# A first layer's weights narrowed by two VectorE instructions with ScalarE's sign, their range check moved into the second layer

## The chip, the core and the metric

One core of a Trainium2 chip runs the whole program. The engines are TensorE (PE; its weight loads, which overlap with the matmuls, are listed as PEld), VectorE (DVE), ScalarE (ACT), GpSimd (POOL) and SyncE (SP), which here only issues DMAs. A q behind an engine's name is its instruction queue. The metric is the time of one execution in microseconds (us).

## What is computed

Complex decaying linear attention over 4 batches, 8 heads, 768 steps and a head size of 48, and then two gated feed-forward layers over the 3072 resulting rows of 384, each with 1536 hidden units; the second normalises its input first.

```
a_re_n, a_im_n = a_re * scale, a_im * scale      # |a| held to 0.999
S_t = a_t * S_(t-1) + k_t v_t^T ;  y_t = q_t . Re(S_t)
x1 = (silu(x @ w_gate) * (x @ w_val)) @ w_out
xn = x1 / sqrt(mean(x1^2) + 1e-6) * rms_g
out = (silu(xn @ w2_gate) * (xn @ w2_val)) @ w2_out
```

The weights come as float64. The kernel takes each as two 32-bit words, makes the float32 number of them ("narrowing"), and splits that into two halves for TensorE, so that a product of two numbers takes three matmuls.

## The kernel before

The sequence is cut into six blocks of 128 steps (512 rows with the four batches). For a block, `e1` and `scan` make the running products of the decays for four heads (a pair of groups), `back`, `e2a` and `e2b` apply them to q and k, and `pe_att` lets TensorE do the transposes (`tp`), scores (`sp`), outputs (`yp`) and the state's update (`zp`) of a group of two heads. When a block's four groups are done, `split_x` splits its rows into `xh` and `xl`, and `layer1` runs the first gated layer on it.

A gated layer goes over 12 blocks of 128 hidden units (`ffn_items`): 9 matmuls into a `gv` buffer for the gate, silu on ScalarE into `h` (line 369), 9 matmuls for the value, the product on VectorE (378), its high half `hh` on ScalarE (379), the low half `hl` on VectorE (387), and then the output's matmuls (`acc` in layer 1, line 792; `o` in layer 2, line 912), one hidden block behind. The `gv` buffers are three.

A hidden block has three weight tiles of 128x384 (gate, value, out), and `load_w` (line 319) prepares each: SP loads the words into `wraw` (two buffers, line 327), `narrow` makes `wy` with three VectorE instructions (lines 59 to 61), ScalarE copies the high half (330) and does the range check, a Square and a Relu that each add up what they find into `wstat` (331, 332). The low half comes from TensorE in layer 1 (`wl`, lines 335 and 336, then a copy, 337) and from VectorE in layer 2 (339). Layer 1's 36 tiles are prepared while the attention of the first blocks runs; layer 2's during the last block of layer 1 and the first of layer 2, since most wait for the space of layer 1's.

The order of the work in the first part is set by due times: each task (`e` for the decays of a pair, `b` for the work on q and k of a group, `t` for its TensorE part, `x` and `f` for split and layer 1 of a block, `w` for a weight tile) has a start and a length in the tables at the top, and `in_order` sorts all items by them. A scheduler then places each engine's instructions, with a priority for the silu, product and halves (`HP`). At the end, `wstat` and other statistics decide whether the plain recurrence has to be run instead (it isn't).

## Time and profile before

| what | value |
|---|---|
| three timed runs, median (range) | 1218.65 us (1217.30 to 1219.31) |
| the profiled execution, span from its first to its last instruction | 1218.1 us |
| TensorE busy | 1136.6 us (93%) |
| its weight loads busy | 945.7 us (78%) |
| VectorE busy | 772.5 us (63%) |
| ScalarE busy | 668.2 us (55%) |
| mean granted TensorE clock | 0.979 of full |

The profiled execution's time outside the span is not listed. A share of busy time is a mean over stages that differ; a line such as "PE wl L335 <- DVE wy L61" says that TensorE's `wl` matmul of line 335 waited for the VectorE instruction of line 61 that writes `wy`.

### The profile page before, as it was taken

The numbers are of one execution on the slowest core, as the hardware profiler recorded it, in microseconds if no ns is written. First come the engines' busy times: TensorE is split into PE (matmuls) and PEld (weight loads), VectorE is DVE, ScalarE is ACT, GpSimd is POOL, SyncE is SP. The second block draws the span as 40 slices with busy tenths as digits, with TensorE's granted clock in tenths as the row PEclk, the third lists the DMA queues.
The fourth block names the chain that finished last, engine by engine and source line by source line (L and its number), as shares of the span: only waits on it lengthen the run. The fifth ranks groups of instructions, "written<-read, shape, count | busy, mean of one in ns | idle before, by whom it ended". The sixth has DMA issues, their size and how long they took to land.

```text
span 1218.1 us, 16677 instructions
## 1 busy us (share of the span) xinstructions
PE 1136.6 (93%) x6098; PEld 945.7 (78%) x6098; DVE 772.5 (63%) x1703; ACT 668.2 (55%) x1159; POOL 1.5 (0%) x12
## 2 busy tenths in 40 slices
PE   2368979999999999999999999999999999999997
PEld 1256767788888888888878887888888888888886
DVE  5997989989898696888754488742422424224222
ACT  5666979877677656675464688742421424214211
POOL 0000000000000000000000000000000000000000
PEclk9877989999999999999999999999999999999999
DMA  6355454432423224232313244400010000000000
GB/s 166 87 138 145 120 151 124 141 110 74 107 77 101 72 63 119 57 85 67 98 59 97 79 130 145 128 26 27 1 52 1 26 26 1 26 1 1 27 1 29
DMA packets 105514, 90.84 MB, mean 75 GB/s; under 512 B 34000, under 2 KB 92368, under 8 KB 105424
## 3 DMA queue, kind: packets, MB, share of 16 engines
q1 hardware_dynamic: 102832, 84.97, 24.8%
q10 hardware_dynamic: 2592, 4.72, 1.0%
q8 instruction: 50, 0.82, 0.3%
q14 instruction: 40, 0.33, 0.1%
HBM read 66.06 MB, written 18.87 MB: 70 GB/s over the span
## 4 chain that ended last, share of the span: by engine, by line
PE 72%; ACT 11%; DVE 8%; DMA 5%; issue 1%; SPq 1%; ACTq 0%; DVEq 0%
PE gv L360 39%; PE o L912 12%; PE acc L792 8%; PE sp L699 4%; PE tp L684 3%; DMA wraw<-in_moe_w_gate_dram 2%; ACT T L690 2%; PE zp L740 2%; PE yp L716 2%; DMA wraw<-in_moe_w_val_dram 2%; PE yp L721 1%; ACT w L331 1%; ACT L420 1%; ACT T L687 1%; ACT w L332 1%
## 5 line engine op out<-in xcount | busy, mean ns | idle before, releaser
L360 PE MATMUL gv<-xh,w 128*128 128x512 f32 x1728 | 571.4, 396 | 0.3 <-ACT h L369 0.3
L360 PEld LDWEIGHTS gv<-xh,w 128*128 128x128 f32 x1728 | 324.6, 188 | 68.7 <-issue 2.1
L360 PE MATMUL gv<-xl,w 128*128 128x512 f32 x864 | 339.5, 393 | 0.0
L378 DVE TENSOR_TENSOR gv<-h,gv 128x512 f32<-128x512 f32 x144 | 99.8, 693 | 225.5 <-PE gv L360 219.5
L369 ACT ACTIVATE h<-gv 128x512 f32<-128x512 f32 x144 | 85.7, 595 | 187.3 <-PE gv L360 186.8
L360 PEld LDWEIGHTS gv<-xl,w 128*128 128x128 f32 x864 | 162.6, 188 | 32.4 <-issue 1.7
L379 ACT ACTIVATE hh<-gv 128x512 fp32r<-128x512 f32 x144 | 85.5, 594 | 166.4 <-DVE gv L378 166.2
L387 DVE TENSOR_TENSOR hl<-gv,hh 128x512 fp32r<-128x512 f32 x144 | 99.1, 688 | 102.3 <-PE o L912 72.5
L792 PE MATMUL acc<-hh,w 128*128 128x512 f32 x432 | 149.0, 399 | 2.4 <-ACT hh L379 2.4
L912 PE MATMUL o<-w,hh 128*128 128x384 f32 x576 | 146.4, 336 | 0.2 <-ACT x1s L798 0.2
L912 PEld LDWEIGHTS o<-w,hh 128*128 128x128 f32 x576 | 105.6, 188 | 5.7 <-ACT x1s L798 0.5
L912 PE MATMUL o<-w,hl 128*128 128x384 f32 x288 | 96.9, 340 | 0.5 <-DVE hl L387 0.5
L792 PEld LDWEIGHTS acc<-hh,w 128*128 128x128 f32 x432 | 80.3, 188 | 21.3 <-ACT hh L379 4.3
L792 PE MATMUL acc<-hl,w 128*128 128x512 f32 x216 | 86.3, 399 | 0.7 <-DVE hl L387 0.7
L335 PE MATMUL wl<-wy,ident 128*128 128x384 f32 x72 | 39.1, 632 | 43.7 <-DVE wy L61 31.5
L690 ACT ACTIVATE T<-tp 96x512 f32<-96x512 f32 x48 | 52.6, 1097 | 43.0 <-PE tp L684 42.6
L699 PEld LDWEIGHTS sp<-T,T 96*128 96x128 f32 x384 | 51.0, 202 | 24.1 <-ACT T L687 22.6
L699 PE MATMUL sp<-T,T 96*128 96x128 f32 x384 | 56.9, 294 | 11.0 <-ACT T L687 10.7
L912 PEld LDWEIGHTS o<-w,hl 128*128 128x128 f32 x288 | 53.6, 188 | 2.6 <-DVE hl L387 2.6
L335 PEld LDWEIGHTS wl<-wy,ident 128*128 128x128 f32 x72 | 14.2, 228 | 51.8 <-DVE wy L61 36.4
L369 ACT ACT_TABLE_LOAD x38 | 48.8, 1283 | 3.4 <-PE gv L360 2.7
L792 PEld LDWEIGHTS acc<-hl,w 128*128 128x128 f32 x216 | 40.6, 188 | 11.1 <-DVE hl L387 2.8
(131 smaller groups left out, 1496.4 us busy)
## 6 DMA issues: line engine op xcount, KB each, us to landing
wraw<-in_moe_w_gate_dram SPq DMA_DIRECT2D x24, 384.0 KB, 3.5
wraw<-in_moe_w_val_dram SPq DMA_DIRECT2D x24, 384.0 KB, 3.5
wraw<-in_moe_w_out_dram SPq DMA_DIRECT2D x24, 384.0 KB, 3.1
kd<-kt SPq DMA_DIRECT2D x24, 384.0 KB, 2.6
ktok<-kd SPq DMA_DIRECT2D x24, 384.0 KB, 3.5
aar<-in_a_re_dram SPq DMA_DIRECT2D x48, 96.0 KB, 2.3
aar<-in_a_im_dram SPq DMA_DIRECT2D x48, 96.0 KB, 2.6
qk<-in_q_dram SPq DMA_DIRECT2D x96, 48.0 KB, 2.4
```

Source lines behind the costliest of these rows:

```text
L335: T.matmul(ps[:, :384], ident, y, start=True, stop=False)
L360: T.matmul(ps[:, :N], w[:, a, i + c, :], x()[b][:, c, :N], start=(n == 0), stop=(n == 8))
L369: A.activation(h[:, :N], st[f, 0][:, :N], AF.Silu)
L378: V.tensor_tensor(t[:, :N], st[f, "h"][:, :N], st[f, 3][:, :N], op=ALU.mult)
L379: A.activation(hh[:, :N], t[:, :N], AF.Copy)
L387: V.tensor_tensor(hl[:, :N], st[f, "t"][:, :N], st[f, "hh"][:, :N].bitcast(F32), op=ALU.subtract)
L684: T.transpose(ps[0:96, u * 128:u * 128 + 128], s[:, u, h].rearrange("p c d -> p (c d)"), ident)
L690: A.activation(t[:, :N].rearrange("p (b r u) -> p u b r", u=U, b=B), ps[0:96, :N].rearrange("p (u b r) -> p u b r", u=U, b=B), AF.Copy)
L699: T.matmul(ps[:C, bb * C:bb * C + C], o[h, 1][:, bb], o[h, 0][:, :, bb, :], start=True, stop=True)
L716: T.matmul(dst, vt[i][:C, col:col + 64], o[h, "p"][:C, bb * C:bb * C + C].rearrange("p (u r) -> p u r", u=U), start=True, stop=not inter)
L792: T.matmul(acc[e][:, :N], w[:, a, 6 + e, :], hs_[c][:, :N], start=(f == 0 and n == 0), stop=(f == NF - 1 and n == 2))
L912: T.matmul(acc[m][:, :DM], hs_[c][:, m * 128:m * 128 + 128], w[:, a, 6:9, :].rearrange("p c e -> p (c e)"), start=(f == 0 and x == 0), sto ...
```

## The change

For layer 1's weights `narrow2` takes the place of `narrow`. ScalarE takes the Sign of the upper word, read as a float, and scales it by -2.0; VectorE then shifts the lower word in with an exclusive or, and the upper word likewise, in two instructions (lines 69 and 70) where there were three. This holds for weights in a known range, which the check has to ascertain.

Layer 1's range check leaves `load_w`. In layer 2, from its second block on, each silu is followed by one check (`check_w`: Square, Relu and a second Relu, each with an accumulated sum), until all 36 tiles are through; for it each tile is loaded a second time (`check_load`), into the `wraw` buffers that are then free. One added VectorE instruction joins the second sum to the first. Layer 2's weights keep `narrow` and their check, which now stands ahead of the high half's copy.

The tables of due times, two lengths, the two priorities (`HP`, `HP_AT`), the place of a late item (`ZAT`), the moment of the first normalisation (`XAT`), that of layer 2's weights (`LAG`), and one table-load setting (`LOGS2`) have new values. Comments are gone.

```
-T_E1 = [-0.615, 0.377, 2.51, 3.055, 4.01, 5, 6.095, 7.158, 8, 9, 10, 10.197]
+T_E1 = [-0.615, 0.377, 2.51, 3.055, 3.906, 5, 6.095, 7.158, 8, 8.14, 10, 10.197]
...
-D_E1 = 1.023
-D_E2 = 1
+D_E1 = 0.801
+D_E2 = 1.049
...
-ZAT = 6
-HP = 140
-HP_AT = 0
+ZAT = 3
+HP = 166
+HP_AT = 33
...
+def narrow2(A, V, raw, y, sg):
+    lo, hi, yu = raw[:, :, 0], raw[:, :, 1], y.bitcast(U32)
+    A.activation(sg, hi.bitcast(F32), AF.Sign)
+    A.activation(sg, sg, AF.Copy, scale=-2.0)
+    V.scalar_tensor_tensor(yu, lo, 29, sg.bitcast(U32), op0=ALU.logical_shift_right, op1=ALU.bitwise_xor)
+    V.scalar_tensor_tensor(yu, hi, 3, yu, op0=ALU.logical_shift_left, op1=ALU.bitwise_xor)
...
+        def range_of(up, lo, dst, n):
+            A.activation(dst, up, AF.Square, accum_out=wstat[:, 0, n:n + 1])
+            A.activation(dst, lo, AF.Relu, scale=-1.0 / LOW ** 2, bias=one, accum_out=wstat[:, 1, n:n + 1])
...
+        def check_w(raw, n):
+            a, t = raw[:, :, 0].bitcast(F32), raw[:, :, 1].bitcast(F32)
+            A.activation(a, t, AF.Square, accum_out=wstat[:, 0, n:n + 1])
+            A.activation(t, a, AF.Relu, scale=-1.0 / LOW ** 2, bias=one, accum_out=wstat[:, 1, n:n + 1])
+            A.activation(t, a, AF.Relu, bias=high, accum_out=wbig[:, n:n + 1])
...
-                    narrow(V, raw, y)
+                    if layer == 0:
+                        narrow2(A, V, raw, y, y)
+                    else:
+                        narrow(V, raw, y)
+                        range_of(raw[:, :, 1].bitcast(F32), lo.bitcast(F32), lo, n)
                     A.activation(hi, y, AF.Copy)
-                    A.activation(lo, raw[:, :, 1].bitcast(F32), AF.Square, accum_out=wstat[:, 0, n:n + 1])
-                    A.activation(lo, lo.bitcast(F32), AF.Relu, scale=-1.0 / LOW ** 2, bias=one, accum_out=wstat[:, 1, n:n + 1])
...
-                fn()
+                r = fn()
+                if n and r is not None:
+                    if ready:
+                        with tc.issue_after(r.ins):
+                            check_w(*ready.pop(0))
...
+                    if todo:
+                        m = todo.pop(0)
+                        ready.append((check_load(m), m))
```

Lines of the changed kernel lie about 32 further down: 486 to 489 are the running products' instructions (454 to 457 before), 363 and 368 the copies of the high half and of `wl` (330 and 337), 400 the silu, 411 the copy to `hh`, 719 and 722 the copies of `tp` (687 and 690), 735 the masked scores `pt` (703).

On VectorE, around the 13th and the 14th narrowed tile, shortly before layer 1's first matmul. Before:

```order
L494 SCALAR_TENSOR_TENSOR e1w_848<-an_847,e1w_848 128x768
L60 SCALAR_TENSOR_TENSOR wy_899<-wraw_900,wy_899 128x384
L59 TENSOR_SCALAR wy_924<-wraw_925 128x384
L61 SCALAR_TENSOR_TENSOR wy_899<-wraw_900,wy_899 128x384
L60 SCALAR_TENSOR_TENSOR wy_924<-wraw_925,wy_924 128x384
L703 TENSOR_TENSOR pt_838<-sp_833,mask4_99 128x512
L499 SCALAR_TENSOR_TENSOR e1w_848<-e1w_848,an_847 128x768
L778 TENSOR_TENSOR xl_917<-xf_506,xh_916 128x512
L502 TENSOR_TENSOR an_847<-aar_714,e1w_848 128x768 x2
L703 TENSOR_TENSOR pt_863<-sp_858,mask4_99 128x512
L747 TENSOR_SCALAR state_108<-zp_867 96x384
L61 SCALAR_TENSOR_TENSOR wy_924<-wraw_925,wy_924 128x384
```

Now:

```order
L486 TENSOR_TENSOR sc1_904<-an_804 128x384
L70 SCALAR_TENSOR_TENSOR wy_892<-wraw_893,wy_892 128x384
L735 TENSOR_TENSOR pt_831<-sp_826,mask4_99 128x512
L779 TENSOR_SCALAR state_108<-zp_833 96x384
L487 TENSOR_TENSOR sc2_905<-an_804 128x384
L782 TENSOR_TENSOR state_108<-state_108,zp_833 96x384
L488 TENSOR_TENSOR an_804<-sc1_904,sc2_905 128x192
L489 TENSOR_TENSOR an_804<-sc1_904,sc2_905 128x192
L810 TENSOR_TENSOR xl_911<-xf_499,xh_910 128x512 x2
L69 SCALAR_TENSOR_TENSOR wy_918<-wraw_919,wy_918 128x384
L735 TENSOR_TENSOR pt_870<-sp_865,mask4_99 128x512
L70 SCALAR_TENSOR_TENSOR wy_918<-wraw_919,wy_918 128x384
```

Each tile has two instructions (69 and 70) in place of three; the split of the block's rows (778, now 810) and the state's update (750, now 782) stand ahead of the 14th tile now, and so does the first part of a running product (486 to 489).

On ScalarE at the same place, around the preparation of the 14th tile. Before:

```order
L330 ACTIVATE w_898<-wy_899 128x384
L690 ACTIVATE T1_845<-tp_840 96x4x128
L687 ACTIVATE T0_855<-tp_850 96x512
L337 ACTIVATE w_898<-wl_908 128x384
L331 ACTIVATE w_898,wstat_63<-wraw_954 128x384
L332 ACTIVATE w_898,wstat_63<-w_898,small_92 128x384
L330 ACTIVATE w_898<-wy_924 128x384
L723 ACTIVATE yt_894<-yp_885 128x512
```

Now:

```order
L67 ACTIVATE wy_918<-wraw_919 128x384
L363 ACTIVATE w_891<-wy_892 128x384
L68 ACTIVATE wy_918<-wy_918 128x384
L722 ACTIVATE T1_853<-tp_848 96x4x128
L368 ACTIVATE w_891<-wl_900 128x384
L719 ACTIVATE T0_860<-tp_855 96x512
L67 ACTIVATE wy_946<-wraw_947 128x384
L68 ACTIVATE wy_946<-wy_946 128x384
L363 ACTIVATE w_891<-wy_918 128x384
```

The check (331, 332) is gone; a Sign (67) and a scaled copy (68) stand ahead of the tile's high half, with copies for the attention and for earlier tiles between them.

On ScalarE in layer 2, at the beginning of its second block. Before:

```order
L369 ACTIVATE h_8065<-gv_8055 128x512
L379 ACTIVATE hh_8077<-gv_8067 128x512
L369 ACTIVATE h_8092<-gv_8082 128x512
L379 ACTIVATE hh_8104<-gv_8094 128x512
L369 ACTIVATE h_8135<-gv_8125 128x512
L379 ACTIVATE hh_8147<-gv_8137 128x512
```

Now:

```order
L400 ACTIVATE h_8062<-gv_8052 128x512
L342 ACTIVATE craw_8035,wstat_63<-craw_8035 128x384
L343 ACTIVATE craw_8035,wstat_63<-craw_8035,small_92 128x384
L344 ACTIVATE craw_8035,wbig_6675<-craw_8035,high_6673 128x384
L411 ACTIVATE hh_8079<-gv_8069 128x512
L400 ACTIVATE h_8110<-gv_8100 128x512
L342 ACTIVATE craw_8067,wstat_63<-craw_8067 128x384
L343 ACTIVATE craw_8067,wstat_63<-craw_8067,small_92 128x384
L344 ACTIVATE craw_8067,wbig_6675<-craw_8067,high_6673 128x384
L411 ACTIVATE hh_8127<-gv_8117 128x512
L400 ACTIVATE h_8154<-gv_8144 128x512
```

Between a silu (400) and the copy to `hh` (411) stand the three instructions of a check on a tile loaded again (`craw`). On SP the first two of these loads stand ahead of the load of the next block's rows, the third behind the four stores of the first block's output, and the others one by one between the later loads and stores.

## Rows read from the trace of the kernel before

**Rows 1.** The page, busy us, share of the span and instructions of each engine.

```profile
PE 1136.6 (93%) x6098; PEld 945.7 (78%) x6098; DVE 772.5 (63%) x1703; ACT 668.2 (55%) x1159; POOL 1.5 (0%) x12
```

**Rows 2.** Busy time by stage (A to E in order): stretch, length, engines, clock, DMA, GB/s.

```profile
0.00:115.40 115.40, 60.18 (x295) 41.94 (x296) 91.92 (x231) 72.23 (x152) 1.32 (x11) 0.82 0.47 129
115.40:245.00 129.60, 118.00 (x652) 91.88 (x652) 120.65 (x315) 107.86 (x225) 0.00 (x0) 0.97 0.49 137
245.00:683.50 438.50, 434.44 (x2685) 360.08 (x2685) 339.01 (x789) 276.77 (x390) 0.20 (x1) 1.00 0.30 84
683.50:790.00 106.50, 103.41 (x459) 84.96 (x459) 85.64 (x173) 85.96 (x210) 0.00 (x0) 1.00 0.44 130
790.00:1218.10 428.10, 420.55 (x2013) 366.86 (x2012) 135.26 (x199) 125.36 (x184) 0.00 (x0) 1.00 0.05 17
```

**Rows 3.** Waits of TensorE in A: total us, times, longest.

```profile
PE wl L335 <- DVE wy L61: 28.8, 7, 13.9
```

**Rows 4.** Waits of TensorE in B.

```profile
PE tp L684 <- DVE X L457: 5.9, 1, 5.9
...
PE wl L335 <- DVE wy L61: 2.7, 2, 1.6
...
PE sp L699 <- ACT T L687: 0.9, 3, 0.3
```

**Rows 5.** Groups by line: shapes, count, busy us, mean ns, idle us before and releaser.

```profile
L387 DVE TENSOR_TENSOR hl<-gv,hh 128x512 fp32r<-128x512 f32 x144 | 99.1, 688 | 102.3 <-PE o L912 72.5 <-ACT hh L379 15.2 <-PE acc L792 14.0
...
L332 ACT ACTIVATE w<-w,small 128x384 fp32r<-128x384 f32 x72 | 44.0, 611 | 0.9
...
L60 DVE SCALAR_TENSOR_TENSOR wy<-wraw,wy 128x384 uint32<-128x384 uint32 x72 | 39.6, 552 | 0.8
...
L331 ACT ACTIVATE w<-wraw 128x384 fp32r<-128x384 f32 x72 | 39.5, 549 | 12.9 <-DMA wraw<-in_moe_w_gate_dram 6.4 <-DMA wraw<-in_moe_w_val_dram 5.2 <-DMA wraw<-in_moe_w_out_dram 1.0
...
L59 DVE TENSOR_SCALAR wy<-wraw 128x384 uint32<-128x384 uint32 x72 | 25.4, 355 | 18.6 <-DMA wraw<-in_moe_w_gate_dram 12.6 <-DMA wraw<-in_moe_w_val_dram 3.5 <-DMA wraw<-in_moe_w_out_dram 2.2
...
L454 DVE TENSOR_TENSOR sc<-X 128x180 f32<-128x180 f32 (+5 forms) x84 | 25.2, 300 | 1.1
...
L454 DVE TENSOR_TENSOR sc<-an 128x384 f32<-128x384 f32 x36 | 19.8, 551 | 0.3
...
L331 ACT ACTIVATION_READ_ACCUMULATOR w<-wraw 128x1 f32 x72 | 13.9, 193 | 0.0
...
L456 DVE TENSOR_TENSOR an<-sc,sc 128x192 f32<-128x192 f32 x24 | 8.4, 350 | 0.1
```

**Rows 6.** VectorE at the second and third narrowing: start us, us, instruction.

```profile
18.29 0.35 DVE L59 TENSOR_SCALAR wy<-wraw 128x384 uint32<-128x384 uint32 x1
18.56 0.55 DVE L61 SCALAR_TENSOR_TENSOR wy<-wraw,wy 128x384 uint32<-128x384 uint32 x1
```

**Rows 7.** ScalarE around a table load.

```profile
703.62 0.51 ACT L330 ACTIVATE w<-wy 128x384 fp32r<-128x384 f32 x1
704.14 1.28 ACT L369 ACT_TABLE_LOAD   x1
705.44 0.60 ACT L369 ACTIVATE h<-gv 128x512 f32<-128x512 f32 x1
```

**Rows 8.** ScalarE in layer 2, a silu and the copy behind it.

```profile
850.90 0.60 ACT L369 ACTIVATE h<-gv 128x512 f32<-128x512 f32 x1 [2.85 <-PE gv L360]
853.68 0.60 ACT L379 ACTIVATE hh<-gv 128x512 fp32r<-128x512 f32 x1 [2.18 <-DVE gv L378]
```

**Rows 9.** The chain that ended last, in layer 2: start us, us, what.

```profile
832.19 8.20 PE gv L360 x36
...
903.56 4.46 PE o L912 x24
...
1205.96 4.48 PE o L912 x24
```

**Rows 10.** DMA issues: count, KB each, median us to landing.

```profile
wraw<-in_moe_w_gate_dram SPq DMA_DIRECT2D x24, 384.0 KB, 3.5
```

More of the change, by code (lines that the diff above doesn't have):

```diff
@@ L24 @@
 UNITS = [4, 4, 4, 4, 4, 4]
-T_E1 = [-0.615, 0.377, 2.51, 3.055, 4.01, 5, 6.095, 7.158, 8, 9, 10, 10.197]
+T_E1 = [-0.615, 0.377, 2.51, 3.055, 3.906, 5, 6.095, 7.158, 8, 8.14, 10, 10.197]
 T_A = [-0.251, 0.965, 2.01, 2.555, 3.95, 4.95, 5.95, 6.95, 7.95, 8.084, 9.939, 10.147]
-T_E2 = [0.533, 1.547, 2.901, 3.934, 4.547, 5.547, 6.547, 6.742, 7.742, 8.742, 9.742, 9.939]
-T_AT = [1.042, 1.872, 3.207, 4.24, 5.042, 5.317, 6.918, 8.042, 9.236, 10.042, 10.704, 10.987]
+T_E2 = [0.533, 1.547, 2.901, 3.934, 4.547, 5.458, 6.547, 6.742, 7.742, 8.742, 9.742, 9.939]
+T_AT = [1.06, 1.877, 3.225, 4.258, 5.06, 5.335, 6.936, 8.06, 9.254, 10.06, 10.722, 11.005]
 T_F = [2.9, 5.616, 7.11, 9.343, 11.118]
-T_X = [2.85, 4.956, 6.956, 8.956, 10.956]
-D_E1 = 1.023
-D_E2 = 1
+T_X = [2.85, 4.956, 6.956, 11.192, 13.192]
+D_E1 = 0.801
+D_E2 = 1.049
 D_AT = 1
 D_F = [2.386, 3.063, 1.974, 1.954, 2.623]
-ZAT = 6
-HP = 140
-HP_AT = 0
+ZAT = 3
+HP = 166
+HP_AT = 33
 BUFS = dict(kt=2, e2t=1, ktok=1, T1=1, T0=2, qt=1, X=1, Xt=2, Ttok=1, qk=2, vt=2, pt=2, md=1, h=1, hh=2, hl=1, yt=2, wy=2, wraw=2)
 EARLY = 1
-LAG = 0.51
-XAT = 3.312
+LAG = 0.5
+XAT = 3.731
 LOGS1 = 2
-LOGS2 = 3
+LOGS2 = 2
 PROD = 1
@@ L314, in decay_attention_two_ffn, with check_load @@
             masks[u] = m
+        def range_of(up, lo, dst, n):
+            A.activation(dst, up, AF.Square, accum_out=wstat[:, 0, n:n + 1])
+            A.activation(dst, lo, AF.Relu, scale=-1.0 / LOW ** 2, bias=one, accum_out=wstat[:, 1, n:n + 1])
+        def check_load(n):
+            raw = wst.tile([128, 384, 2], U32, tag="wraw", name="craw", bufs=BUFS["wraw"])
+            dst = raw.rearrange("p n t -> p (n t)")
+            f, i = divmod(n, 3)
+            SY.dma_start(out=dst if i == 2 else dst.rearrange("p (c f) -> p c f", c=NC),
+                         in_=words((wg, wv, wo)[i], f, i == 2))
+            return raw
+        def check_w(raw, n):
[3 more added lines that the diff above has]
+            A.activation(t, a, AF.Relu, bias=high, accum_out=wbig[:, n:n + 1])
         def load_w(w, srcs, f, layer, which=(0, 1, 2)):
@@ L368, in go @@
                     with tc.high_priority(HP):
-                        A.activation(h[:, :N], st[f, 0][:, :N], AF.Silu)
+                        r = A.activation(h[:, :N], st[f, 0][:, :N], AF.Silu)
                     st[f, "h"] = h
+                    return r
                 return go
@@ L931, in decay_attention_two_ffn @@
         G.memset(ones, 1.0)
+        high = ff2.tile([128, 1], F32, name="high", bufs=1)
+        G.memset(high, -3.9999997)
+        wbig = ff2.tile([128, 3 * NF], F32, name="wbig", bufs=1)
         wx = fast.enter_context(tc.tile_pool(name="wx", bufs=EARLY))
@@ L957, in decay_attention_two_ffn @@
             nf_ += 1
+        todo, ready = list(range(3 * NF)) if wg.dtype == U32 else [], []
         for n in range(nb_):
@@ L963, in decay_attention_two_ffn @@
                     x2[n + 1] = norm(512 * (n + 1))
-                fn()
+                r = fn()
[3 more added lines that the diff above has]
+                            check_w(*ready.pop(0))
+                        if not ready and not todo:
+                            V.tensor_tensor(wstat[:, 1, :3 * NF], wstat[:, 1, :3 * NF], wbig, op=ALU.add)
+                    if todo:
+                        m = todo.pop(0)
+                        ready.append((check_load(m), m))
     with tc.tile_pool(name="fl", bufs=1) as fl_, tc.tile_pool(name="fps", bufs=1, space=PSUM) as fps:
```

## The prediction

> **What bounds the kernel now.** Over the whole span TensorE is busy 93% and VectorE 63% [rows 1]. That average hides stages, so I read the busy time by stage next [rows 2]. Stage A (0 to 115.4 us) ends with the first matmul of layer 1, B (to 245 us) covers the rest of the first block of layer 1 and the last of its weights, C (to 683.5) the other blocks, D (to 790) the loading of layer 2's weights, E the rest. TensorE's idle time is the stage less its busy time: A 115.4 - 60.2 = 55.2 us, B 129.6 - 118.0 = 11.6, C 438.5 - 434.4 = 4.1, D 106.5 - 103.4 = 3.1, E 7.6, all of it behind the last matmul, since the chain of waits runs through layer 2 on TensorE alone and its last matmul ends at 1205.96 + 4.48 = 1210.4 [rows 9]. So from 245 us on the kernel is TensorE's, and time can be won nearly only in A and B, 66.8 us of idle time.
>
> Who keeps TensorE waiting there? In A its waits for a narrowed weight (`wy`, line 61) are the largest item, 28.8 us in 7 waits [rows 3]; VectorE is busy 91.9 of 115.4 us [rows 2]. In B VectorE is busy 120.7 of 129.6 us, TensorE 118.0 and ScalarE 107.9 [rows 2]: VectorE is the densest, TensorE close behind. TensorE's listed waits in B end with VectorE for the most part: 5.9 (line 457), 2.7 (the narrowing), against 0.9 for ScalarE's copies [rows 4].
>
> **What the change moves, and its price.** *VectorE.* Each of layer 1's 36 weights loses the 0.355 us instruction of line 59; the two that remain have the form of line 60, 0.552 us [rows 5]. That is 36 x 0.355 = 12.8 us. The true gain of one lies between 0.27 (the distance from its start to the next start when it runs back to back, 18.29 to 18.56 [rows 6]) and 0.355: 9.7 to 12.8 us for all. I take the upper end, because line 60 needs its result and often stands next to it.
>
> The due times are new, so I compare VectorE's order up to the same two instructions. Up to the 14th narrowing (both orders put 14 weights ahead of layer 1's first matmul): 14 x 0.355 = 5.0 us less, but one more step of running products (lines 454 to 457, 2 x 0.55 + 2 x 0.35 = 1.8 us [rows 5]) and two small ones (lines 750 and 546, at most 1.1, I take 0.7) more: **-2.5 us**. Up to the 36th: 12.8 less, ten of the running products' instructions more (at most 0.30 each, 3.0) and one 0.69 us subtraction (line 387) less [rows 5]: -12.8 + 3.0 - 0.7 = **-10.5 us**, so -8.0 of it in B. The matmuls ahead of these points are the same but for about one attention step.
>
> A then starts layer 1 earlier by 2.5 us (between 0, if another chain than VectorE's ends last, and 5.0). In B VectorE's 120.7 us fall to 112.7, below TensorE's 118.0. The two change places, so not all 8.0 can be kept: VectorE will wait more for TensorE. The floor is 118.0 plus the waits that ScalarE causes (0.9 and some tenths), about 119.5, so at most 129.6 - 119.5 = 10 us could go; I take three quarters of 8.0, **-6.0** (ends 0 and -10).
>
> *ScalarE.* A weight's range check (lines 331 and 332 with two reads of the accumulator, 0.549 + 0.611 + 2 x 0.193 = 1.55 us) goes, Sign and a scaled Copy come. No row shows Sign on this form; the nearest are Copy on 128x384 (0.51 [rows 7]) and Square (0.549 [rows 5]); I take 0.52 for each, as both are near the Copy: 1.04 us, so 36 x 0.5 = 18 us less (17 to 19 by the two ends). The new order has 6 more table loads (90 for 84), 5 of them ahead of the 12th silu. A load takes 1.28 us and the next instruction starts 1.30 us after it, while the one ahead ended as it began (703.62 + 0.51, then 704.14 [rows 7]): 6 x 1.3 = 7.8 us. ScalarE is left with about 10 us less in A and B, so I cost this at nothing. The Trainium skill says it otherwise ("ScalarE: Activation LUTs", section What ACT_TABLE_LOAD costs): a switch is the load and a drain of about 1.38 us, 2.66 in all. By that, six would cost 16 us and ScalarE would be left with some 2 us less; the sum would stay, with no cushion. The rows here show no drain, and I go by them. The Sign, however, stands ahead of VectorE's first narrowing instruction, a new wait (a rival below).
>
> *Layer 2's weights (D).* The range check moves ahead of the high half's copy, and can run while VectorE narrows. The work is the same; at stake are the 3.1 us of idle time. I take 0 (ends -3 and +2).
>
> *The check in layer 2 (E).* It adds 36 loads of 384 KB on SP (3.5 us to landing [rows 10]) and 108 instructions behind 36 silus of the layer's second to fifth block, about 0.549 + 2 x 0.611 + 3 x 0.193 = 2.35 us each time. Queued behind them on ScalarE is the copy to `hh`. Now it starts 853.68 - 850.90 = 2.78 us after the silu starts, 2.18 us after it ends, because VectorE's product comes first [rows 8]. So `hh` is late by at most 0.2 us, and its matmuls come only after the next 18 `gv` matmuls, 4.1 us (half of the 8.20 for 36 [rows 9]). At a block's end there is no such cover (24 `o` matmuls in a row [rows 9]), but 12 of the 24 still come first, half of 4.46 us. Each load is issued about two silus ahead, 12 us, except behind the output's stores at a block's end. Cost: 0. If that cover failed, the three block ends that have checks on both sides would lose up to a landing each, 3 x 3.5 = 10.5 us.
>
> **Sum.** -2.5 - 6.0 = -8.5 us. The profiled execution's span is 1218.1 us; the median of the runs shown is 1218.65, 0.6 more, with what lies around the span. The sum is set against the latter: 1218.65 - 8.5 = **1210.2 us**. I call no change what is within 0.2% (2.4 us).
>
> **Rivals.** *1. TensorE is the bound already, and nothing is gained.* TensorE's 118.0 us in B are 91% of the stage, and its longest wait there, 5.9 us, is one stall in the attention chain [rows 4], which shorter narrowing need not shorten. Then only the 2.7 us of B's waits for narrowed weights shrink, by a quarter (0.355 of 1.46): 1218.0 us. The Trainium skill argues this way ("Perfetto Trace Analysis", section Identifying the Most-Contended Engine): work first on the engine with the highest occupancy, judging TensorE by its weight loads; over the span these are busy 78%, VectorE 63%. The same page allows for regimes in which the engine changes. Against the rival stand the narrowing's 28.8 us in A [rows 3] and VectorE's 93% of B [rows 2]. Chance 0.17.
>
> *2. Sign holds up VectorE, and it gets slower.* ScalarE runs in order, with 107.9 of B's 129.6 us busy, and a Sign that stands behind a late copy or a late load makes VectorE, the densest engine, wait. The gain is gone when a weight's narrowing waits 0.355 us longer on average. With half of Sign and Copy exposed (0.52) it is 36 x (0.52 - 0.355) = +5.9 us: 1224.6 us; all exposed, +24.7. For it: both are new links in the chain from load to narrowed weight, 1.04 us against the 0.355 saved. Against it: in the new order VectorE has other work between most of them, and Sign needs only the load, as the Square of line 331 did, and a free `wy` buffer, as line 59 did. Chance 0.09.
>
> *3. The check's loads come late in layer 2* and give the gain back, up to 10.5 us as above: 1210.2 + 10.5 = 1220.7 us. Chance 0.04.
>
> **How the numbers follow.** The forecast, VectorE's relief shows in A and B, has 0.70. Its ends are -5.0 - 10 = -15 (1203.7 us) and a loss of most of it (about 1215). The range goes from there up to 1217.5, past the forecast's end into the first rival; what is left out is the rest of the three rivals and the tail below, some 2 in 10. Faster: the forecast and 0.06 of rival 1 (with part of B's gain) and 0.02 of rival 3, 0.78. Same: 0.10 of rival 1 and 0.01 each of 2 and 3, 0.12. Slower: 0.08 of rival 2, 0.01 each of 1 and 3, 0.10.
>
> **What would show it.** Right: the first `gv` matmul of layer 1 starts at about 113 us, the last narrowing ends some 8.5 us earlier than now, VectorE's share of B falls below TensorE's, and from there to the end every stage keeps its length. The instructions that take the place of lines 60 and 61 show about 0.55 us, Sign and Copy about 0.52, and no table load stands in front of a Sign. Layer 2's blocks still take 75.8 us each (from 832.19 to 903.56 + 4.46 [rows 9]), with no hole on TensorE. Wrong: VectorE's narrowing waits for ScalarE by more than 0.355 us a weight; the first matmul comes no earlier; holes in front of `o` matmuls at the block ends; or TensorE's idle time of B reappears in C, in front of the attention's matmuls.

## The result, and the profile after

| | before | after |
|---|---|---|
| timed runs, median (range), us | 1218.49 (1217.30 to 1219.31), 4 runs | 1236.52 (1234.94 to 1237.57), 4 runs |
| ratio after to before, 95% interval | | 1.0142 [1.0122, 1.0163] |

The change makes the kernel 18.0 us slower, where 8.5 us less were forecast; the range ended at 1217.5. The page after, busy time by engine:

```profile
PE 1150.9 (93%) x6098; PEld 950.7 (77%) x6098; DVE 766.2 (62%) x1668; ACT 739.5 (60%) x1309; POOL 1.6 (0%) x13
```

VectorE does less work (772.5 to 766.2 us, with 36 instructions fewer and one more, beside [rows 1]). TensorE has the same 6098 matmuls and is busy 14.3 us longer. To see where, here is the busy time by stage after, cut at the matmuls of [rows 2] (B's end within 0.7 us, D's within 1.4) (stretch, length, TensorE, weight loads, VectorE, ScalarE, GpSimd, clock, DMA share, GB/s):

```profile
0.00:121.85 121.85, 65.12 (x294) 45.28 (x295) 91.90 (x224) 70.79 (x123) 1.32 (x11) 0.96 0.45 125
121.85:250.60 128.75, 116.68 (x649) 91.11 (x649) 115.34 (x292) 106.44 (x181) 0.00 (x0) 0.97 0.48 136
250.60:697.00 446.40, 441.39 (x2689) 362.53 (x2688) 337.09 (x783) 280.11 (x397) 0.24 (x2) 1.00 0.29 82
697.00:805.30 108.30, 105.22 (x468) 86.41 (x467) 85.67 (x170) 86.24 (x211) 0.00 (x0) 1.00 0.44 135
805.30:1235.40 430.10, 422.50 (x2005) 365.42 (x2003) 136.22 (x202) 195.96 (x399) 0.00 (x0) 0.99 0.15 48
```

A is 6.5 us longer, though VectorE is no busier in it; B only 0.9 us shorter (1.6 by the same matmul), though VectorE has 5.3 us less; C 7.9 us longer (8.6 by the same matmul) with hardly more idle time, 5.0 us for 4.1; D and E together 3.8 us longer.

*A.* TensorE's idle time there is 56.7 us after and 55.2 before, 1.5 more; its busy time is 4.9 us more. The waits in A, of TensorE before (beside [rows 3]), then of TensorE and VectorE after (engine, line, what was waited for, total us, times, longest):

```profile
PE wl L335 <- DVE vt L449: 12.1, 1, 12.1
...
PE tp L684 <- DVE kt L659: 3.9, 3, 3.1
PE tp L684 <- ACT T L690: 1.2, 1, 1.2
```

```profile
PE wl L366 <- DVE wy L70: 37.6, 7, 16.4
PE tp L716 <- DVE kt L691: 7.5, 3, 3.9
...
PE tp L716 <- ACT T L722: 4.9, 4, 1.5
...
DVE wy L69 <- ACT wy L68: 4.0, 3, 2.6
```

By these names TensorE's wait for narrowed weights rose from 28.8 us [rows 3] to 37.6. But TensorE's very first wait, for the first weight, is listed before under `vt` (12.1 us) and after under `wy` (13.4 us). Counted alike, the wait is 40.9 us before and 37.6 after: it became 3.3 us shorter, as it was to. What rose is the wait of the attention's transposes, for `kt` and for ScalarE's copies `T`, from 5.1 to 12.4 us. TensorE in the middle of A, before and then after (start us, us, instruction, idle time before it):

```profile
60.83 1.97 PE L716 MATMUL yp<-pt,vt 128*64 128x128 f32 x14 [1.18 <-DVE pt L703]
...
70.82 1.06 PE L684 MATMUL tp<-ident,kt 128*96 128x128 f32 x4
...
74.47 1.16 PE L699 MATMUL sp<-T,T 96*128 96x128 f32 x8 [1.13 <-ACT T L687]
75.47 0.80 PE L740 MATMUL zp<-vt,ktok 128*96 128x48 f32 x8
```

```profile
58.15 1.97 PE L748 MATMUL yp<-pt,vt 128*64 128x128 f32 x14 [0.17 <-DVE pt L735]
...
72.31 1.41 PE L772 MATMUL zp<-vt,ktok 128*96 128x48 f32 x8
...
77.17 1.06 PE L716 MATMUL tp<-ident,kt 128*96 128x128 f32 x4
...
81.15 2.08 PE L731 MATMUL sp<-T,T 96*128 96x128 f32 x8 [0.68 <-ACT T L719]
```

After is 2.7 us ahead at the outputs (`yp`) and 6.3 us behind at the transposes (`tp`): the state's update (`zp`) now stands ahead of these transposes, before it stood behind them and the next scores (`sp`). The busy time grew since more of A's matmuls have their longer length: single `sp` matmuls take about 0.28 or about 0.43 us, and 43 of A's 64 are over 0.35 us after, 36 before. The 4th and the 6th narrowing are 13 and 15 us late in A, but they are 14 and 12 us late in c2_check_alone below too, and A is 1.2 us shorter there. So they aren't what makes A longer.

*B.* The waits of TensorE and VectorE after:

```profile
PE wl L366 <- DVE wy L70: 8.3, 2, 6.9
...
DVE wy L69 <- ACT wy L68: 1.5, 2, 1.2
```

The wait for narrowed weights rose from 2.7 us to 8.3, while the 5.9 us for `X` [rows 4] are gone; TensorE's idle time in B is 12.1 us, for 11.6 before. VectorE itself waited for the scaled Copy only 5.5 us in A and B, 0.15 us a weight. So the narrowing came late without VectorE standing still: it was put later in VectorE's order. The timeline after around the longest of B's waits, first ScalarE, then VectorE, then TensorE:

```profile
147.35 0.98 ACT L67 ACTIVATE wy<-wraw 128x384 f32<-128x384 f32 x2
...
152.64 0.55 DVE L69 SCALAR_TENSOR_TENSOR wy<-wraw,wy 128x384 uint32<-128x384 uint32 x1
...
153.58 0.55 DVE L70 SCALAR_TENSOR_TENSOR wy<-wraw,wy 128x384 uint32<-128x384 uint32 x1
...
154.19 1.65 PE L366 MATMUL wl<-wy,ident 128*128 128x384 f32 x2 [6.91 <-DVE wy L70]
```

This is the 19th weight. The Sign for the 18th starts at 132.54; the next Sign stands on ScalarE 14.8 us later, at 147.35, behind attention work, and VectorE comes to the 19th at 152.64. Before, its last narrowing instruction started at 131.8 us; the 19th to the 24th are all 20 to 26 us late. The Sign need not be the reason: with the new tables and no Sign (e2 and c3 below) the same six are 12 to 31 us late.

*C.* No wait explains the loss. The groups that grew most, before and then after (line, shapes, count, busy us, mean ns):

```profile
L716 PE MATMUL yp<-pt,vt 128*64 128x128 f32 x272 | 30.7, 282 | 0.0
L721 PE MATMUL yp<-T,state 96*64 96x128 f32 x272 | 29.8, 273 | 0.0
```

```profile
L748 PE MATMUL yp<-pt,vt 128*64 128x128 f32 x272 | 33.8, 283 | 0.0
L753 PE MATMUL yp<-T,state 96*64 96x128 f32 x272 | 32.5, 273 | 0.0
```

The same 544 `yp` matmuls, each with the same mean, cover 5.8 us more. They come in 17 groups of 32, whose matmuls overlap one another: a group in one piece takes 1.97 us from its first start to the start of what follows, one cut by other matmuls into 4 and 28 takes 0.58 + 1.91 = 2.49. Before, two of the 17 are cut, after, ten are; 8 x 0.52 = 4.2 us, and the sum of these times rises from 34.5 to 38.7. Such a cut after (`gv` stands inside the group):

```profile
275.82 0.43 PE L748 MATMUL yp<-pt,vt 128*64 128x128 f32 x2
276.09 0.38 PE L753 MATMUL yp<-T,state 96*64 96x128 f32 x2
276.40 0.73 PE L391 MATMUL gv<-xh,w 128*128 128x512 f32 x2
...
277.30 0.45 PE L748 MATMUL yp<-pt,vt 128*64 128x128 f32 x4
```

All seven kernels with the new tables, or with the order made by them, have ten to twelve cut groups in C, all others two. That is half of C's loss; the rest is spread over the other kinds of matmul.

*Layer 2.* The last loss is there, in the chain of waits after (start us, us, what), beside [rows 9]:

```profile
918.33 4.46 PE o L944 x24
922.79 8.29 PE gv L391 x36
...
1223.23 4.47 PE o L944 x24
```

36 `gv` matmuls take 8.29 us, not 8.20, and from the first of these `o` groups to the last it is 304.9 us where it was 302.4: 0.6 us a block, some 3.7 us over six blocks, evenly, with and without checks.

### The profile page after: what moved, and what is told of

Its sections match the earlier page's. It is cut to its first block, busy times and chain, and to the rows that moved or that the text cites. A ratio compares the mean times of both kernels' runs of the same rounds, so it can differ in the third digit from the quotient of the medians.

```text
span 1235.4 us, 16828 instructions
## 1 busy us (share of the span) xinstructions
PE 1150.9 (93%) x6098; PEld 950.7 (77%) x6098; DVE 766.2 (62%) x1668; ACT 739.5 (60%) x1309; POOL 1.6 (0%) x13
## 3 DMA queue, kind: packets, MB, share of 16 engines
q1 hardware_dynamic: 114160, 99.13, 27.8%
## 4 chain that ended last, share of the span: by engine, by line
PE 77%; ACT 10%; DVE 7%; DMA 3%; issue 2%; SPq 1%; ACTq 0%; DVEq 0%
PE gv L391 41%; PE o L944 12%; PE acc L824 8%; PE sp L731 4%; PE tp L716 3%; PE zp L772 2%; PE yp L748 2%; ACT T L722 2%; PE wl L366 2%; PE yp L753 1%; DMA wraw<-in_moe_w_val_dram 1%; DMA wraw<-in_moe_w_gate_dram 1%; ACT L452 1%; ACT L400 1%; ACT T L719 1%
## 5 line engine op out<-in xcount | busy, mean ns | idle before, releaser
L824 PEld LDWEIGHTS acc<-hh,w 128*128 128x128 f32 x432 | 80.6, 188 | 21.8 <-ACT hh L411 5.4
L731 PEld LDWEIGHTS sp<-T,T 96*128 96x128 f32 x384 | 52.1, 206 | 21.9 <-ACT T L719 20.7
L735 DVE TENSOR_TENSOR pt<-sp,mask 128x512 f32<-128x512 f32 x48 | 33.0, 688 | 35.4 <-PE sp L731 35.2
```

The costliest lines, as they stand in the source:

```text
L731: T.matmul(ps[:C, bb * C:bb * C + C], o[h, 1][:, bb], o[h, 0][:, :, bb, :], start=True, stop=True)
L735: V.tensor_tensor(t[:C, :N].rearrange("p (b c) -> p b c", b=B), ps[:C, :N].rearrange("p (b c) -> p b c", b=B), m, op=ALU.mult)
L824: T.matmul(acc[e][:, :N], w[:, a, 6 + e, :], hs_[c][:, :N], start=(f == 0 and n == 0), stop=(f == NF - 1 and n == 2))
```

## The experiments

**How the stages are compared.** For each run the table gives how much later than in the profile of before the same matmul starts, in us: the first `gv` of layer 1 (end of A), the 200th (end of B), the 1109th (C), the 1405th (D); then the start of the last `o` group (1205.96 before), and the timed ratio. One profile strays from another by a few us: the last but one column lies within 6 us of the timed difference, mostly below it. Only larger jumps, or equal ones in several runs, are read.

| run | A | B | C | D | last `o` | timed ratio |
|---|---|---|---|---|---|---|
| after | +6.5 | +4.9 | +13.5 | +13.9 | +17.3 | 1.0142 [1.0122, 1.0163] |
| e1_old_tables | +9.4 | +22.2 | +28.5 | +29.6 | +33.1 | 1.0255 [1.0236, 1.0274] |
| e2_new_tables | +9.6 | +9.1 | +33.6 | +36.5 | +36.5 | 1.0306 [1.0280, 1.0332] |
| e3_pad192 | -0.1 | -1.4 | -1.5 | +0.1 | +3.6 | 1.0027 [1.0016, 1.0038] |
| e4_no_check | +7.7 | +5.8 | +14.3 | +15.3 | +15.3 | 1.0121 [1.0096, 1.0146] |
| c1_narrow2_alone | +3.9 | +22.2 | +22.1 | +21.9 | +21.8 | 1.0203 [1.0166, 1.0239] |
| c2_check_alone | -1.2 | -6.1 | +0.6 | +0.6 | +4.0 | 1.0053 [1.0033, 1.0073] |
| c3_three_instr | +6.5 | +0.1 | +16.9 | +18.0 | +21.4 | 1.0219 [1.0191, 1.0248] |
| g1_hpat0 | +1.9 | +12.0 | +25.9 | +26.6 | +30.0 | 1.0305 [1.0267, 1.0343] |
| k1_narrow2_f0 | -7.4 | +20.1 | +36.4 | +35.9 | +35.9 | 1.0317 [1.0293, 1.0340] |
| k2_after_f0 | -3.4 | +6.1 | +26.6 | +28.5 | +31.9 | 1.0273 [1.0249, 1.0297] |
| d1_no_line59 | -2.2 | +6.4 | +14.6 | +16.8 | +16.8 | 1.0141 [1.0111, 1.0171] |
| p1_pad160 | -1.0 | -2.0 | -2.1 | -1.7 | +2.2 | 1.0045 [1.0028, 1.0062] |
| x1_narrow2_same_order | +8.0 | +28.3 | +28.3 | +27.8 | +27.8 | 1.0237 [1.0220, 1.0254] |
| x2_both_same_order | -1.3 | +12.5 | +12.5 | +12.3 | +12.4 | 1.0132 [1.0115, 1.0149] |
| x3_no59_same_order | +2.7 | +5.7 | +6.2 | +6.2 | +6.1 | 1.0066 [1.0049, 1.0082] |
| x4_old_work_new_order | +5.7 | +7.5 | +16.1 | +17.5 | +17.5 | 1.0180 [1.0140, 1.0221] |
| x5_placed_by_hand | -1.2 | +2.5 | +2.6 | +2.6 | +2.7 | 1.0069 [1.0052, 1.0087] |
| x6_no59_all_queues | -2.3 | -3.6 | -3.7 | -3.7 | -3.4 | 1.0006 [0.9994, 1.0018] |

### The halves of the change

**e1_old_tables**: the new work with the old tables.

```
-T_E1 = [-0.615, 0.377, 2.51, 3.055, 3.906, 5, 6.095, 7.158, 8, 8.14, 10, 10.197]
+T_E1 = [-0.615, 0.377, 2.51, 3.055, 4.01, 5, 6.095, 7.158, 8, 9, 10, 10.197]
...
```

The other eleven settings go back likewise.

> The changed kernel with the due times, lengths and priorities of the kernel before; narrow2 and the check in layer 2 stay. In the changed kernel's trace the first gv matmul comes 6.1 us later than before, the last block of layer 1 begins 13.1 us later, and layer 2 adds another 3.5 us by stretching every block from 75.8 to 76.4 us. Theory D (the new tables cost what is lost ahead of layer 2): the first gv matmul is back at 115 us or earlier, about 1222 us or less (1236.5 - 13 - some of VectorE's relief). Theory S (the Sign and the scaled Copy on ScalarE hold up the narrowing): still 6 us late at the first gv, 1231 us or more.

**e2_new_tables**: the kernel before with the twelve new settings, nothing else.

> The kernel before with the new due times, lengths and priorities alone; three narrowing instructions and the check stay where they were. Theory D: slower by about what is lost ahead of layer 2, 1218.5 + 13 = 1231 us, layer 2's blocks at 75.8 us. Theory S: 1218 to 1222 us, since without a Sign nothing new is in the chain to a narrowed weight.

Measured: 1249.74 and 1256.59 us, against 1217.47 on the same chip. Each half by itself is worse than the whole, 2.6% and 3.1% against 1.4%. So work and tables can't be priced apart and added, and neither half holds the gain.

**c1_narrow2_alone**: the old tables, `narrow2` for layer 1, the check where it was.

```
-                    narrow(V, raw, y)
+                    if layer == 0:
+                        narrow2(A, V, raw, y, y)
+                    else:
+                        narrow(V, raw, y)
```

> The kernel before with narrow2 for layer 1's weights and nothing else: range check in its old place, old due times and priorities, old addresses. Theory F (the due times and priorities only fit the work they were made with, and any change of the early instructions' order costs, whatever work it saves): slower by 10 us or more, 1228 us or above, although VectorE has 12.8 us less to do. Theory S (it is the Sign's place in ScalarE's queue): also slower, and then PE's and VectorE's waits end with lines 67 and 68. The prediction's own reckoning (VectorE's relief is worth something): 1205 to 1215 us.

**c2_check_alone**: the old tables, three instructions, the check moved into layer 2 as in the change.

```
-                        narrow2(A, V, raw, y, y)
+                        narrow(V, raw, y)
```

> The kernel before with layer 1's range check moved into layer 2 and nothing else: three narrowing instructions, old due times and priorities. ScalarE loses 36 x 1.55 us ahead of layer 2. Layer 2's tiles stand 192 bytes further, which the pad alone priced at 3.8 us: 1221.3 us if nothing else changes. Theory F: 1230 us or more, with the loss in layer 1. Theory S: 1217 to 1222 us, since no Sign is there.

**c3_three_instr**: the same edit in the changed kernel, new tables kept.

> The changed kernel with its new due times and its check in layer 2, but layer 1's weights narrowed by the three VectorE instructions of before, without a Sign. Theory S: faster than the changed kernel, 1225 us or less. Theory F: the new tables were made with narrow2 in place, so without it 1240 us or more, though ScalarE has 36 x 1.07 us less to do. If VectorE's work is what counts: 1236.5 + 8 to 13 = 1245 to 1249 us.

Measured: 1242.51, 1224.70 and 1243.91 us, against 1217.16. `narrow2` alone costs 2%, all of it by the end of B; the check alone costs 0.5%, and its profile shows 3.4 us of that behind D. In the new tables the two-instruction form is better than the three-instruction one, 1.0142 against 1.0219. (One of c1's four executions took 3968.63 us; it is not in the ratio, and its cause is open.) TensorE in the middle of B in c1 (start us, us, instruction, idle time before it), and its stretches from there:

```profile
158.44 1.05 PE L696 MATMUL tp<-ident,kt 128*96 128x128 f32 x4 [4.13 <-DVE kt L671]
```

```profile
150.00:170.00 20.00, 11.56 (x50) 8.97 (x49) 14.01 (x23) 13.92 (x27) 0.00 (x0) 0.71 0.24 70
170.00:190.00 20.00, 17.47 (x86) 13.28 (x86) 14.63 (x43) 14.64 (x25) 0.00 (x0) 0.78 0.43 114
190.00:210.00 20.00, 19.28 (x133) 15.55 (x132) 14.54 (x41) 19.40 (x40) 0.00 (x0) 1.00 0.46 133
```

Behind the hole the attention's matmuls run without layer 1's between them, and the granted clock is 0.71 and 0.78 for 40 us before it is back at 1.00; eight `sp` take 2.08 us at 161.16, where at the full clock they take 1.16 (74.47 before). Here a wait in B cost its own length and slower matmuls behind it.

**g1_hpat0**, **k1_narrow2_f0** and **k2_after_f0** each turn one setting (the second one in c1, the others in the changed kernel).

```
-HP_AT = 33
+HP_AT = 0
...
-T_F = [2.9, 5.616, 7.11, 9.343, 11.118]
+T_F = [2.7, 5.616, 7.11, 9.343, 11.118]
...
-T_F = [2.9, 5.616, 7.11, 9.343, 11.118]
+T_F = [2.5, 5.616, 7.11, 9.343, 11.118]
```

> The changed kernel with one number taken back: the priority of the masked scores, 33 to 0. In the changed kernel VectorE waits 9.4 us for scores ahead of the first gv matmul (before: 2.8), and the state's and the scores' matmuls of the later blocks take 4.2 us more. If this number causes these two: 1236.5 - 6 - 4 = 1226 us. Theory F: one number taken back from tables made together gives 1236 us or more.

> The kernel before with narrow2 alone (as in the earlier run, which took 1242.5 us), and one due time more: layer 1's first block is due at 2.7 in place of 2.9. Theory G: what costs is the place of the second block's first attention group in TensorE's queue. In the kernel before, and in the two fast ones, 90 gv matmuls stand ahead of that group's first tp; with narrow2 alone it is 72, and TensorE waits there for kt and then runs the group by itself at a low clock. The earlier due time puts 90 there again. By theory G the time comes back by more than half of the 25 us lost: 1230 us or less, and the hole in front of that tp goes. By theory F (any change of one number costs): 1242 us or more.

> The changed kernel with the first block of layer 1 due at 2.5 in place of 2.9, which puts 90 gv matmuls ahead of the second block's first tp (54 in the changed kernel). Theory G: the 6.9 us wait for the 19th narrowed weight and its low clock shrink, 1230 us or less. Theory F: 1236 us or more.

Measured: 1252.82 (against 1217.16), 1256.62 and 1252.50 us (against 1218.06). All three are slower than what they were made from. Starting layer 1 earlier does give an earlier A (-7.4 and -3.4), and B and C lose 30 to 44 us again. So `HP_AT` by itself is not what lengthens C, and the theory that the number of `gv` matmuls ahead of the second block decides falls.

### Layer 2

**e3_pad192** adds to the kernel before nothing but an unused tile of the size of `high` and `wbig` together, at the same place; **p1_pad160** has 40 in place of 48.

```
+        pad = ff2.tile([128, 48], F32, name="pad", bufs=1)
+        G.memset(pad, 0.0)
```

> The kernel before with one unused tile of 192 bytes per partition in layer 2's pool, which puts layer 2's tiles (x1, xh2, xl2, the first weight, os) at the addresses that they have in the changed kernel. Theory L (the addresses stretch layer 2's matmuls): layer 2's blocks take 76.4 us in place of 75.8, 1222 us. Theory K (the check's loads and instructions in layer 2 stretch them): 75.8 us, 1218.5 us.

> The kernel before with an unused tile of 160 bytes per partition in layer 2's pool, in place of the 192 bytes that cost 3.8 us. It tells whether any shift costs (theory: the old addresses happen to be good, 1220 to 1222 us) or whether it depends on the address (xh2 and xl2 now begin at multiples of 256 bytes; 1214 to 1218 us).

**e4_no_check** takes the check and both tiles out of the changed kernel.

```
-                r = fn()
...
+                fn()
```

> The changed kernel without the check in layer 2: layer 1's weights are not range-checked at all, no second load, no tiles high and wbig (so layer 2's tiles stand where they stood before). Theories L and K both say that layer 2's blocks fall back to 75.8 us: 1236.5 - 3.5 = 1233 us, with nothing changed ahead of layer 2. If the blocks stay at 76.4 us, neither the check nor the addresses are the cause of the stretch.

Measured: 1221.29 (+3.8 us), 1223.00 (+4.9) and 1233.38 us. The chain in layer 2, of e3 and then of e4:

```profile
904.64 4.43 PE o L912 x24
909.07 8.29 PE gv L360 x36
...
1209.52 4.46 PE o L912 x24
```

```profile
918.83 4.45 PE o L943 x24
923.28 8.20 PE gv L390 x36
...
1221.23 4.46 PE o L943 x24
```

An unused tile gives 8.29 us and 304.9 us, as the change does; without the two tiles it is 8.20 and 302.4 again. 108 more ScalarE instructions and 36 loads cost layer 2 nothing that can be seen: e3, without them, is as long as the change, and x2 and x5 below, which have them with the two tiles behind all others, take 75.8 us a block as before. The 3.8 us are the addresses of the tiles that lie behind the two new ones, among them `xh` and `xl`, which move by 192 bytes in each partition. Which addresses are good, and why, stays open; 160 bytes are no better.

### What does any change do to the order?

**d1_no_line59** only removes work: line 59 in both layers.

```
-    V.tensor_scalar(yu, hi, 3, 0x3FFFFFF8, op0=ALU.logical_shift_left, op1=ALU.bitwise_and)
-    V.scalar_tensor_tensor(yu, hi, 0xC0000000, yu, op0=ALU.bitwise_and, op1=ALU.bitwise_or)
+    V.scalar_tensor_tensor(yu, hi, 0xC0000000, hi, op0=ALU.bitwise_and, op1=ALU.bitwise_or)
```

> The kernel before without the instruction of line 59: the narrowing keeps its two other VectorE instructions, so no word is shifted by three and the weights are other numbers than the reference's. No ScalarE instruction is added, the check stays, and TensorE's order is nearly that of before (87 gv matmuls ahead of the second block's first tp, 90 before). This is VectorE's relief by itself, for both layers' weights (72 x 0.355 = 25.6 us in all, 12.8 in layer 1). The prediction's sum for the same relief was -8.5 us: 1206 to 1211 us. If VectorE's relief buys nothing because TensorE is the bound: 1216 to 1218 us.

Measured: 1234.82 us against 1218.06, 1.4% slower with 72 instructions (25.4 us, [rows 5]) less on VectorE and nothing added. The scheduler had made the order anew: of the instructions that both kernels share, at least 192 of 1559 on VectorE, 176 of 1075 on ScalarE and 158 of 6098 on TensorE stand elsewhere. VectorE's waits in B of d1, for instance, which is 8.6 us longer there:

```profile
DVE e1w L488 <- ACT e1w L487: 4.4, 2, 4.1
```

Before, this wait in B is 0.7 us.

The next six kernels hold an order fixed instead: each instruction of an engine is tied to the one that shall stand ahead of it, which orders without a wait.

```
+        for _a, _b in zip(_o, _o[1:]):
+            tc.add_manual_dep(_in[_b], _in[_a].name, _dep, reason="order")
```

**x4_old_work_new_order**: the work of before (`narrow`, check in `load_w`) with TensorE, VectorE and ScalarE in the order of the changed kernel.

> The kernel before's work (three narrowing instructions, the check in its old place, no added tiles) in exactly the order of the changed kernel. Theory O: slow like the changed kernel, 1232 to 1245 us (1236.5 less 3.7 for the addresses, plus up to 12.8 for VectorE's work). Theory W: 1217 to 1222 us.

**x3_no59_same_order**: layer 1 without line 59, in the order of before on these three engines; **x6_no59_all_queues**: SyncE's loads in the order of before as well.

```
-                    narrow(V, raw, y)
+                    if layer == 0:
+                        narrow1(V, raw, y)
```

> The kernel before without line 59 in layer 1 (the words are not shifted, so the weights are other numbers than the reference's), every other instruction in exactly the order of before. Removing work from queues whose order is fixed can hardly cost. Theory O: VectorE's relief as the prediction counted it, 1206 to 1213 us. If TensorE is the bound anyway: 1216 to 1218 us. 1225 us or more would speak against O.

> The kernel before without line 59 in layer 1 (so the weights are other numbers than the reference's), with every queue in exactly the old order, SyncE's too. The run without that took 1225.7 us and lost 3.3 us to the fourth weight's load and 4.7 us further on. If SyncE's order was the cause: no slower than before, 1208 to 1218 us, and what is missing to 1218 is VectorE's relief by itself. If it is still 1222 us or more, removing work costs by itself in this order.

Measured: x4 1237.94 and x3 1225.65 us against 1218.22; x6 1217.87 against 1217.37. The stages of x4, A to C:

```profile
0.00:121.10 121.10, 61.17 (x294) 41.14 (x295) 95.78 (x240) 74.33 (x153) 1.32 (x11) 0.83 0.45 128
121.10:253.20 132.10, 117.62 (x649) 91.53 (x649) 119.95 (x313) 111.33 (x224) 0.00 (x0) 0.96 0.45 130
253.20:700.00 446.80, 441.90 (x2690) 362.61 (x2689) 337.05 (x783) 280.39 (x397) 0.20 (x1) 1.00 0.29 82
```

The old work in the new order has A and C as long as the change has them (121.1 and 446.8 us, against 121.85 and 446.4), and C's 441.9 us of TensorE. So A's and C's loss is the order's, not that of Sign or `narrow2`: the state's update stands ahead of the same transposes, and ten groups of `yp` are cut, as in the change. SyncE was not held in x4, but 531 of its 547 transfers stand as in the change. B is 3.3 us longer than after, which may be what the new work gives back there.

x6 is the clean test of the first part of the forecast: 36 times line 59 less, everything else in its place. The time moves by +0.06% [-0.06, +0.18], nothing. (No run holds the order of before with all of its work, so a cost of the ties isn't measured by itself; C, where nothing else changed, is 437.7 us in x6 and 437.8 before.) B of x6:

```profile
113.00:242.00 129.00, 117.74 (x660) 91.34 (x658) 117.05 (x295) 108.39 (x225) 0.00 (x0) 0.97 0.48 138
```

In B VectorE's busy time falls by 3.6 us and the stage by 0.6 (1.3 by the same matmul). The rest is idle time in small pieces, the largest item 3.3 us for TensorE's scores, and TensorE is as busy as before. x3 differs from x6 only in SyncE's order, and is 7.4 us slower than before: its first gate loads keep VectorE waiting 12.4 us in A, in two waits, where x6 has one of 7.9. The order of the loads counts like that of the engines.

### Sign in the order of before

**x1_narrow2_same_order**: `narrow2` with the check in place, in the order of before, Sign and Copy wherever the scheduler lets them in. **x2_both_same_order**: the whole new work so, its two tiles behind all others. **x5_placed_by_hand**: x2, SyncE's order fixed, and each Sign and Copy put behind its load by hand.

```
+                _seq[_pairs[_k]:_pairs[_k]] = [_by[FREE["s"][2 * _k]], _by[FREE["s"][2 * _k + 1]]]
```

> narrow2 alone, the check in its old place, as in the run that took 1242.5 us, but TensorE, VectorE and ScalarE issue every other instruction in exactly the order of the kernel before: the two narrowing instructions stand where lines 60 and 61 stood, Sign and Copy stand where the scheduler puts them. Theory O (the order is what costs): 1206 to 1217 us, VectorE's relief less what 38 us more of ScalarE's work take back. Theory W (the new work costs, a Sign that holds up VectorE): 1225 us or more.

> All of the changed kernel's work (narrow2, the check in layer 2 from a second load) in exactly the order of the kernel before, and the two added tiles placed behind layer 2's other tiles, so that these keep their old addresses. Theory O: the prediction's sum was right for this order: 1206 to 1213 us, faster than both kernels. Theory W: 1225 us or more, since the work is the changed kernel's.

> The changed kernel's work in the order of the kernel before, as in the run that took 1234.2 us, with two things more held: SyncE's transfers are in the old order (the check's loads come on top), and each Sign with its scaled Copy directly behind it stands on ScalarE at the first place after the load has landed and the buffer is free in the trace of before, which is 0.4 us or more ahead of the start of line 60 there. Theory S (what costs is the Sign's place in ScalarE's queue): VectorE's waits for line 72 fall from 16.4 us to under 4 and the time to 1206 to 1215 us, faster than both kernels. Theory V (any new link costs, wherever it stands): 1225 us or more.

Measured: x1 1247.16 and x2 1234.15 us against 1218.22, x5 1224.47 against 1217.37. VectorE's waits for the scaled Copy in B, of x2 and then of x5:

```profile
DVE wy L74 <- ACT wy L72: 16.4, 7, 5.8
```

```profile
DVE wy L75 <- ACT wy L72: 1.7, 5, 0.8
```

The longest in x2, ScalarE's rows and then VectorE's:

```profile
145.47 0.55 ACT L71 ACTIVATE wy<-wraw 128x384 f32<-128x384 f32 x1
...
147.50 1.28 ACT L464 ACT_TABLE_LOAD   x1
...
152.21 1.28 ACT L412 ACT_TABLE_LOAD   x1
...
154.00 0.51 ACT L72 ACTIVATE wy<-wy 128x384 f32<-128x384 f32 x1
...
154.54 0.56 DVE L74 SCALAR_TENSOR_TENSOR wy<-wraw,wy 128x384 uint32<-128x384 uint32 x1 [5.76 <-ACT wy L72]
```

Between a Sign at 145.47 and its Copy at 154.00 lie ten other instructions and two table loads, and VectorE, in order, waits 5.76 us. x1, which has the check on ScalarE as well, loses 8.0 us in A and 20.3 in B; x2 loses nothing in A and 13.8 in B. Placing the pairs by hand takes 14.7 us of such waits out of B, and the timed ratio falls from 1.0132 to 1.0069; SyncE's order was fixed in the same step, so the two are not parted. What is left, 7.1 us, is not traced to a row. x5 is the best of the versions with `narrow2`; none of the 18 is faster than the kernel before.

## Why the prediction was wrong

- **The step that failed: "The due times are new, so I compare VectorE's order up to the same two instructions."** It priced the new order by what VectorE has to do ahead of the 14th and the 36th narrowing, and took "The matmuls ahead of these points are the same but for about one attention step" for proof that nothing else moved. Their number is the same, their order isn't: in A the state's update stands ahead of the next transposes, and in C ten of 17 groups of `yp` are cut, where two were. x4, with none of the new work, shows the price: +5.7 us in A, +8.6 in C, +17.5 by the end of D, 1.8% in all.
- **A, -2.5.** It came +6.5. In the old order the profile shows something of it at most (x6 -2.3, x2 and x5 about -1.3; but e3 and p1, with nothing changed in A, show -0.1 and -1.0), and no timed run shows a gain. VectorE's term itself was too big: 36 times line 59 less is 7.5 us of its busy time over the span in x6 (764.95 us), 0.21 us each and not 0.355, since neighbours overlap. The 28.8 us of waits for narrowed weights, the argument against rival 1, were 40.9 with the first. They did shrink, by 3.3, and A grew all the same: TensorE waited 7.3 us more for the attention and was busy 4.9 us longer.
- **B, -6.0 of 8.0.** It came -1.6 from the first `gv` to the 200th in after, and -1.3 in x6, where the order is the old one. "Three quarters" was a choice with no row behind it. Rival 1 said this: TensorE and the attention chain bound B already. The Trainium skill's rule ("Perfetto Trace Analysis", section Identifying the Most-Contended Engine), read over the span, points to TensorE (its weight loads 78%, VectorE 63%) and was the better guide; read in B alone it points to VectorE (93%, against 71% for the weight loads [rows 2]), and there x6 speaks against it: it lightens that engine, and the time stays.
- **C, nothing.** It came +8.6. The forecast took 4.1 us of idle time for all that could change there. That bounds a gain; it bounds no loss, since TensorE's busy time for the same matmuls is not fixed (434.4 to 441.4 us); the cut groups of `yp` are 4.2 us of it.
- **ScalarE, nothing.** Sign took 0.551 us and the Copy 0.522, forecast 0.52 each; the second Relus 0.64, forecast 0.611. The table loads are 90, as counted, 1.283 us each, and none is at a Sign's line. Sizes were right. Rival 2 asked the right question (does Sign's place hold up VectorE?) and is borne out in the old order, 16.4 us in x2. In the change itself the wait is 0.15 us a weight, below the 0.355 from which it was to decide. Whether the Sign moved the narrowing instead is not shown: it stands late in e2 and c3 too, which have no Sign.
- **The check in layer 2, nothing; rival 3.** Right: no holes, and e3 without the check is as long. What was not among the terms is the address shift, +3.8 us.
- **The sum** was -8.5. By the profiles it is +17.5 for the order (x4), -3.6 for the new work in that order (+13.9 by the end of D, not +17.5) and +3.4 for the addresses: 17.3, against 18.0 timed. The -3.6 is within the few us by which profiles stray; timed, x4 (1.0140 to 1.0221) and the change without its tiles, e4 (1.0096 to 1.0146), are hardly apart. In A the waits and rows above show where the time goes, in C the cut groups show half of it; which of the new settings moves these matmuls is open.

## What to carry to other kernels

Where a scheduler makes the order, a change of work or of its tables is first a new order: compare the order on each engine, first on the one that bounds (here the attention's matmuls on TensorE), not the sums ahead of two points, and price order and work apart by holding the order fixed. A busy share of 93% of a stage doesn't show that lightening the engine shortens it; one kernel that leaves the instruction out in the old order does. Put added small tiles behind the large ones, so that the operands' addresses stay.

## What the runs showed of the hardware

- The spacing of matmuls depends on where their operands lie. In the last block of layer 2 the median distance from one `gv` matmul to the next is 227 ns before and without the two tiles, 232 with the change, 231 with 192 unused bytes and 234 with 160.
- Removing work can cost as much as adding it: 25.4 us of VectorE's instructions less made the kernel 16.8 us slower (d1), while 36 of the 72 less in the old order (x6) moved the time by nothing.
- Cutting a run of small matmuls costs: 32 `yp` in one piece take 1.97 us, in two pieces of 4 and 28 they take 2.49.
- The clock of A's stage rows, 0.96 after and 0.82 before, can't be compared. The trace of after has no clock record ahead of 86.9 us, and its rows show 1.00 there; yet eight `sp` take 2.08 us at 81.15, as they do before at 0.50, 1.2 GHz (2.02 us at 69.01), and not the 1.16 us that they take at 1.00, 2.4 GHz (74.47).
